# Branches on the number of blocks, put in another order with a hint ahead of each far jump, in an attention, mixture-of-experts and MLP kernel

## The chip, the cores and the metric

The kernel runs on one core of a Trainium2 chip. The metric is the device time of one execution in microseconds (us); of several runs the median counts. The engines are named as the profile names them: PE (TensorE, matrix products), ACT (ScalarE), DVE (VectorE), POOL (GpSimd), SP (SyncE, which here issues the DMA transfers). A `q` behind an engine's name is its sequencer, which runs branches, loads of registers and waits.

## What is computed

Three stages, each fed by the one before, all in float32: attention of 2 x 8 heads over 576 positions with a learned bias by position; a layer of eight experts, of which each of the 1152 tokens goes to one; and a last MLP over all tokens. Cut to what matters for the change:

```python
def _moe_ref(x, w_gate, w1, w2, capacity):      # x (1152, 512), E = 8, F = 1024, capacity 288
    ...
    expert_idx = np.argmax(logits, axis=1)
    gate_w = probs[np.arange(N), expert_idx]
    ...
    for i in range(N):
        e = expert_idx[i]
        if counts[e] < capacity:
            disp[e, counts[e]] = x[i]
            ...
            keep[i] = True
    h = np.maximum(np.einsum('ecd,edf->ecf', disp, w1), 0.0)
    y = np.einsum('ecf,efd->ecd', h, w2)
    out = np.zeros((N, D), dtype=np.float32)
    for i in range(N):
        if keep[i]:
            out[i] = gate_w[i] * y[expert_idx[i], pos[i]]

def _moe2_ref(x, w_in, w_out):                  # 512 -> 2048 -> 512
    h = x @ w_in
    g = np.maximum(0.01 * h, h)
    return g @ w_out
```

A token that its expert has no room for has a row of zeros in the output: these are the blank rows.

## The kernel before

One function, `tile_attention_moe_mlp`, records the instructions of all engines in the order in which it is written; each engine runs its own in that order, and where two engines meet, one waits on a semaphore. PE takes a float32 matrix in two halves: `P[:, 0]` is the value rounded by ACT (L676), `P[:, 1]` what is left (L677, by DVE or POOL), and each product is three matmuls (L860, L861, L862).

After attention the tokens are sorted by expert and cut into blocks: big ones of `CAPB` = 288 tokens and small ones of `CAPS` = 64. How many of each there are depends on the tokens, so their number is read at run time, from `ints`, as `ends[0]` (the end of the bigs) and `ends[1]` (the end of the smalls). The input timed has two big blocks and one small one.

A big block is eight calls of `big_step` (L1041), four for the first product of the expert and four for the second. Step j converts the weight tile of step j + 2 (`split`, L1038, by way of `wsplit`, L675) and runs the 24 matmuls of its own tile. An expert has eight weight tiles of 512 KB, which SP loads (`wdma`, L672) into the buffers R8[0] to R8[7] (`raw` and `w` in the trace). Block 0 stands in a straight line (the loop from L1153). In its last step the tokens of the next blocks, `xr` and `xsr`, are transposed on PE (`prep_at`).

Behind block 0, SP issues three transfers of 768 KB that write zeros from the tile `pre` over all of `out` (`prefill(out, ...)`, L1157 and L1158, by way of L150). Then all engines load `ends` (L1159) and branch:

- L1160, `ends[0] > 1`: into `big(1)`, else past it. `big(i)` (L1055) is a recursion that is unrolled when the program is built: `If(ends[0] > i + 1)` (L1058) holds the eight steps of block i as a middle one and, inside, the whole of `big(i + 1)`; its `Else` (L1067) holds the steps of block i as the last big one, which also load the first small expert. For two big blocks L1058 is false for i = 1, and the engines jump over the code of all longer cases to the `Else` of the outermost nest.
- L1162, `ends[1] > ends[0]`: into `small(0)` (L1074), which has the same form with L1129. For one small block L1129 is false for i = 0, and the engines jump over the nest again.

POOL needs no wait before these branches and takes them early; PE, ACT, DVE and SP each come to them when their own work is done.

Then comes the last MLP, `chunk(0)`: its weights, `wo`, come in 16 tiles of 1 MB as 64-bit numbers (`w<-wo`, L684, 13 loads there), DVE turns each to float32 in three steps (L690, L692, L694), and ACT and POOL split them like the experts'. A loop over i from 0 to 12 runs the products; at its end `emit` multiplies by the gate and POOL scatters the rows to `out` (L1197).

Of the kernel before, what the change touches and what calls it, by code (L numbers as in the profile page):

```python
# [51 lines left out]
NLST = 17  # L52
# [22 lines left out]
def tile_attention_moe_mlp(ctx, tc, qc, kc, vc, wpk, cst, ctok, cap, wm, wo, out):  # L75
    nc = tc.nc
# [20 lines left out]
    R8 = CS[:, S // 4 : S // 4 + S // 16]  # L97
# [574 lines left out]
    def wdma(src, raw):  # L672
        nc.sync.dma_start(raw, src)
# [44 lines left out]
    def wsrc(e, j):  # L718
        return wm[bass.ds(e, 1), j].rearrange("a p f -> p (a f)")
# [103 lines left out]
    def tail_part(fa):  # L823
# [151 lines left out]
        def bval(l, i, f, engines):  # L975
            o = 3 * (NLST * l + i) + (2, 0, 1)[f]
            return nc.values_load(blk[0:1, o : o + 1], engines=engines, min_val=0, max_val=(E_N - 1, SROWS - CAPB, T - 1)[f])
# [3 lines left out]
        def load_x(base):  # L981
            for t, n in xtiles:
                nc.sync.dma_start(xr[t][0:n], srt[sl_(base + 128 * t, n), 0:DM])
# [68 lines left out]
            if prep and j >= 5:  # L1052
                prep_x(j - 5)

        def big(i):  # L1055
            xbase, base = bval(0, i, 1, [SP]), bval(0, i, 2, [ACT, DVE, SP])
            copy_id(xbase, base, CAPB)
            with tc.If(ends[0] > i + 1) as more:  # L1058
                if i + 2 < NLST:
                    ne = bval(0, i + 1, 0, [SP])  # L1060
                    load_x(bval(0, i + 1, 1, [SP]))
                    for j in range(8):
                        big_step(j, base, nc.gpsimd, prep=True)
                        for q in ((), (), (0, 1), (2, 3), (4,), (5,), (6,), (7,))[j]:
                            wdma(wsrc(ne, q), R8[q])
                    big(i + 1)
            with more.Else():  # L1067
                ne = bval(1, 0, 0, [SP])
                for j in range(8):
                    big_step(j, base, nc.gpsimd)  # L1070
                    if j > 2:
                        wdma(wsrc(ne, j - 3), R8[j - 3])

        def small(i):  # L1074
            e, xbase, base = bval(1, i, 0, [SP]), bval(1, i, 1, [SP]), bval(1, i, 2, [ACT, DVE, SP])
            for q in (5, 6, 7):
                wdma(wsrc(e, q), R8[q])
            copy_id(xbase, base, CAPS)
            pend_h = []

            def turn():
                j, hb = pend_h.pop()
                pt = gs[gi[0] % 3]
                gi[0] += 1
                for a in range(2):
                    nc.tensor.matmul(pt[:, CAPS * a : CAPS * a + CAPS], hb[:, 128 * a : 128 * a + 128], II, start=True, stop=True)
                v = pt[:, 0 : 2 * CAPS].rearrange("p (a n) -> p a n", a=2)
                d = hs[:, 2 * j : 2 * j + 2]
                nc.scalar.activation(d[:, :, 0:CAPS], v, AF.Relu)
                nc.vector.scalar_tensor_tensor(out=d[:, :, CAPS:], in0=v, scalar=0.0, in1=d[:, :, 0:CAPS].bitcast(F32),  # L1090
                                               op0=ALU.max, op1=ALU.subtract)

            def step(j, last):
                if j < 6 or not last:
                    split((j + 2) % 8, nc.gpsimd if j in SG else nc.vector)
                Pt = Ps[j % 4]
                if j < 4:
                    ps = gs[gi[0] % 3][:, 0:256]
                    gi[0] += 1
                    for k in range(NP):  # L1100
                        for t in range(2):
                            nc.tensor.matmul(ps, xsh[:, k], Pt[:, t, 256 * k : 256 * k + 256], start=k + t == 0, stop=k == NP - 1 and t == 1)
                    nc.scalar.copy(hsb[j % 2], ps)
                    if pend_h:
                        turn()
                    pend_h.append((j, hsb[j % 2]))
                else:
                    for kk in range(2):
                        k = 2 * (j - 4) + kk
                        for t in range(2):  # L1110
                            for i in range(2):
                                o = 512 * kk + 256 * i
                                nc.tensor.matmul(acs[i][:, 0:256], hs[:, k], Pt[:, t, o : o + 256], start=k + t == 0, stop=k == 7 and t == 1)
                    if j == 4:
                        turn()

            def finish(last):
                nc.scalar.copy(ysb[:, 0:256], acs[0][:, 0:256])
                nc.vector.tensor_copy(ysb[:, 256:512], acs[1][:, 0:256])
                for i in range(2):  # L1120
                    ps = gs[gi[0] % 3]
                    gi[0] += 1
                    for k in range(2):
                        nc.tensor.matmul(ps[:, CAPS * k : CAPS * k + CAPS], ysb[:, 256 * i + 128 * k : 256 * i + 128 * k + 128], II, start=True, stop=True)
                    nc.vector.tensor_copy(y[:, 2 * i : 2 * i + 2, sl_(base, CAPS)], ps[:, 0 : 2 * CAPS].rearrange("p (k n) -> p k n", k=2))
                if last:
                    yprep(0)

            with tc.If(ends[1] > ends[0] + i + 1) as more:  # L1129
                if i + 2 < NLST:  # L1130
                    ne = bval(1, i + 1, 0, [SP])
                    load_xs(bval(1, i + 1, 1, [SP]))
                    for j in range(8):
                        step(j, False)
                        if j > 2:
                            wdma(wsrc(ne, j - 3), R8[j - 3])
                        if j == 6:
                            prep_xs()
                    finish(False)
                    small(i + 1)  # L1140
            with more.Else():
                for j in range(8):
                    step(j, True)
                finish(True)

        fa = fa[:2] + fin_b(*fa)
        run(fill(mb[:, 0], kbt[0:nr, :, 1], kbt[0:nr, :, 1], ALU.add))
# [2 lines left out]
            for t in PX[m + 1]:  # L1150
                prep_xs() if t == 3 else prep_x(t)

        for j in range(8):  # L1153
            big_step(j, 0, nc.vector, post0, last=prep_at)
            if j == 6:
                prep_at(-1)
        for i in range(3):  # L1157
            prefill(out, 3 * i, 3)  # L1158
        ends = [nc.values_load(ints[0:1, 4 + i : 5 + i], min_val=0, max_val=2 * NBLK) for i in range(2)]  # L1159
        with tc.If(ends[0] > 1):  # L1160
            big(1)
        with tc.If(ends[1] > ends[0]) as more:  # L1162
            small(0)
        with more.Else():
            yprep(0)

        osb = [rt.tile([128, DM], F32, name=f"osb{i}", tag="xn", bufs=XB) for i in range(-(-MC // 128))]
        kt = nc.values_load(ints[0:1, 1:2], min_val=0, max_val=T)
# [31 lines left out]
        def chunk(c):  # L1200
            w = MCS[c]
            groups = [(t, min(128, w - 128 * t)) for t in range(-(-w // 128))]
            cv = convs()
            PP = [Ds[i] if c == 0 and i < 2 else Ps[i % 4] for i in range(16)]
            if c:
                for i in range(3):
                    wdma(wsc[i], raws[i])
                yprep(c)
            for i in range(3, 5):
                conv_start(i)  # L1210
            if c:
                for i in range(2):
                    wsplit(raws[i], PP[i], nc.vector)
            for i in range(13):
                if i + 2 < 16:
                    wsplit(spare if c == 0 and i == 0 else raws[(i + 2) % 4], PP[i + 2], nc.gpsimd)
                q = PO[i]
                if q < 8:
                    for g in (0, 2, 1, 3):
                        up_half(PP[i], 2 * q + g // 2, w // 2 * (g % 2), w // 2)  # L1220
                        if g != 3:
                            next(cv, None)
                else:
                    for kk in range(2):
                        for t, n in groups:
                            down_tok(PP[i], 2 * (q - 8) + kk, t, n)
                            if t == 0:
                                split_h()
                            if 2 * t + kk in DCV:
                                next(cv, None)  # L1230
                if i == 5:
                    for t, n in groups:
                        nc.sync.dma_start(idg[0:n, t], sid[MOF[c] + 128 * t : MOF[c] + 128 * t + n].bitcast(I32))
            wsplit(raws[15 % 4], PP[15], nc.vector)
            for t, n in groups:
                for i in range(13, 16):
                    for kk in range(2):
                        down_tok(PP[i], 2 * (PO[i] - 8) + kk, t, n)
                emit(t, n)
# [114 lines left out]
```

## Time and profile before

| | us |
|---|---|
| median of 3 runs | 423.31 |
| lowest and highest | 421.41, 426.03 |
| span of the profiled execution, first to last instruction | 422.7 |
| its busy PE, DVE, ACT, POOL | 384.0, 307.7, 241.3, 138.3 |

One page describes one execution. Busy time is what an engine's instructions took; branches, waits and the issuing of transfers are not counted in it. The views behind the page say more: a list of an engine's waits names the instruction that waited and what released it ("issue" where nothing that the profile shows did); the rows of a source line give the length of each kind of instruction of that line, branches (COMPARE_BRANCH) too; a timeline gives the instructions of an engine with the idle time ahead of each in brackets; windows give busy time, granted TensorE clock (1.00 is the 2.4 GHz level) and DMA traffic of chosen stretches. Matmuls overlap in the pipeline, so the distance of their starts, and not their length, says how fast they run.

### The profile page before, as it was taken

How to read it: one execution, taken by the hardware profiler on the slowest of the kernel's cores; microseconds unless marked ns; L12 is line 12 of the kernel's file. 1: busy time of each engine (PE TensorE's matmuls, PEld its weight loads, DVE VectorE, ACT ScalarE, POOL GpSimd, SP SyncE). 2: the span in 40 equal slices, each digit the busy share in tenths (PEclk: the TensorE clock that was granted, in tenths of full speed). 3: DMA queues.
4: the chain of work that ended last, by engine and by line, in shares of the span. 5: the costliest groups of instructions: out<-in, count | busy, mean ns of one | idle time of the engine just before them, and what ended most of it. 6: DMA issues, size and time to landing. Idle time of an engine off the chain costs nothing. (4 is left out here: it accounts for less than half of the span.)

```text
span 422.7 us, 8338 instructions
## 1 busy us (share of the span) xinstructions
PE 384.0 (91%) x2926; PEld 317.9 (75%) x2926; DVE 307.7 (73%) x731; ACT 241.3 (57%) x519; POOL 138.3 (33%) x110
## 2 busy tenths in 40 slices
PE   4877999998999999999999976997999999999995
PEld 2235566566788888988889966996888877988783
DVE  5997888798855789799458940205799899999500
ACT  3746898697865877767655852526554512455300
POOL 1443857374100101212332202780122245242221
PEclk9998899999899999999999996999999999999999
DMA  8989498698678938788364469850523356640011
GB/s 202 344 236 309 156 346 303 215 304 257 177 213 302 316 125 258 203 258 241 70 204 189 152 218 362 281 195 6 200 100 101 115 185 200 211 188 2 0 68 54
DMA packets 34371, 83.10 MB, mean 197 GB/s; under 512 B 8479, under 2 KB 8863, under 8 KB 32260
## 3 DMA queue, kind: packets, MB, share of 16 engines
q1 hardware_dynamic: 33188, 79.88, 58.6%
q0 software_dynamic: 1120, 2.48, 1.7%
q8 instruction: 28, 0.46, 0.5%
q14 instruction: 35, 0.29, 0.2%
HBM read 60.29 MB, written 23.20 MB: 197 GB/s over the span
## 5 line engine op out<-in xcount | busy, mean ns | idle before, releaser
L345 DVE CUSTOM_DVE_ANT_0 sv<-St,bt 128x576 f32<-128x576 f32 x72 | 52.9, 751 | 36.0 <-PE St L333 24.1
L677 POOL TENSOR_TENSOR P<-raw,P 128x1024 fp32r<-128x1024 f32 x18 | 45.6, 2535 | 81.6 <-ACT P L676 81.5
L356 ACT ACTIVATE A<-sv,mx 128x576 f32<-128x576 f32 x72 | 59.2, 837 | 3.9 <-DVE mx L345 3.7
L333 PE MATMUL St<-K,Q 128*128 128x320 f32 (+1 forms) x320 | 55.0, 316 | 3.2 <-DVE mx L345 3.2
L333 PEld LDWEIGHTS St<-K,Q 128*128 128x128 f32 x320 | 45.5, 195 | 15.1 <-issue 10.2
L182 PE MATMUL pb<-Gt,WP 128*32 128x272 f32 (+17 forms) x352 | 44.0, 504 | 14.0 <-DVE Gt L165 7.8
L273 POOL TENSOR_TENSOR Q<-qr,Q 128x256 fp32r<-128x256 f32 x22 | 17.1, 777 | 105.9 <-ACT Q L265 64.5
L676 ACT CAST P<-raw 128x1024 fp32r<-128x1024 f32 x27 | 28.3, 1048 | 36.8 <-DVE raw L694 22.7
L165 DVE TENSOR_SCALAR Gt<-WL,bp 128x432 f32<-128x432 f32 (+17 forms) x101 | 48.4, 539 | 0.1
L366 PE MATMUL pt<-CS,A 128*128 128x128 f32 x288 | 42.1, 287 | 0.4 <-ACT bs L193 0.2
L376 ACT COPY AT<-pt 128x512 f32<-128x512 f32 x40 | 23.4, 585 | 32.2 <-PE pt L366 32.1
L366 PEld LDWEIGHTS pt<-CS,A 128*128 128x128 f32 x288 | 38.7, 207 | 1.0 <-ACT bs L193 0.4
L182 PEld LDWEIGHTS pb<-Gt,WP 128*32 128x32 f32 x352 | 13.1, 111 | 31.7 <-DVE Gt L165 14.6
L169 POOL TENSOR_SCALAR Gt<-WL,bp 128x528 f32<-128x528 f32 (+12 forms) x17 | 33.8, 1993 | 9.3 <-PE pb L182 9.2
L403 PE MATMUL xp<-AT,V 128*64 128x128 f32 x512 | 36.2, 285 | 0.0
L193 ACT ACTIVATE bs<-pb,CS 128x288 f32<-128x288 f32 (+53 forms) x60 | 27.4, 504 | 12.8 <-PE pb L182 8.3
L860 PE MATMUL g<-yhl,P 128*128 128x304 f32 x96 | 30.2, 315 | 3.8 <-DVE gfa L885 3.8
L1189 PE MATMUL ac<-P,hq 128*128 128x512 f32 (+1 forms) x80 | 31.5, 394 | 0.0
L1187 PE MATMUL ac<-P,hq 128*128 128x512 f32 (+1 forms) x80 | 31.5, 394 | 0.0
L1188 PE MATMUL ac<-P,hq 128*128 128x512 f32 (+1 forms) x80 | 31.5, 393 | 0.0
L403 PEld LDWEIGHTS xp<-AT,V 128*64 128x64 f32 x512 | 28.3, 140 | 4.0 <-issue 0.2
L893 DVE TENSOR_TENSOR hq<-gfa,hq 128x304 fp32r<-128x304 f32 x32 | 28.7, 897 | 1.4 <-ACT hq L892 1.4
(317 smaller groups left out, 909.3 us busy)
## 6 DMA issues: line engine op xcount, KB each, us to landing
bt<-scr SPq DMA_DIRECT2D x24, 576.0 KB, 4.8
w<-wo SPq DMA_DIRECT2D x13, 1024.0 KB, 4.9
scr<-bs SPq DMA_DIRECT2D x36, 295.5 KB, 5.1
raw<-wm SPq DMA_DIRECT2D x14, 512.0 KB, 6.7
w<-wm SPq DMA_DIRECT2D x10, 512.0 KB, 5.8
srt<-pre SPq DMA_DIRECT2D x6, 771.0 KB, 7.8
qr<-qc SPq DMA_DIRECT2D x16, 256.0 KB, 5.6
kr<-kc SPq DMA_DIRECT2D x12, 288.0 KB, 6.7
```

The source lines that it names most:

```text
L165: nc.vector.tensor_scalar(G, src, bp[:, g : g + 1], 0.0, op0=ALU.add, op1=ALU.max)
L169: nc.gpsimd.tensor_scalar(G, src, bp[:, g : g + 1], 0.0, op0=ALU.add, op1=ALU.max)
L182: nc.tensor.matmul(pb[32 * q : 32 * q + 32, 0 : hi - lo], W2, gs[:, q, lo:hi], start=True, stop=True)
L333: nc.tensor.matmul(St[:, o + lo : o + hi], Q[:, h - 2 * p, w, :], K[:, h - 2 * p, lo:hi], start=n == 0, stop=n == len(seq) - 1)
L345: nc.vector.tensor_tensor_reduce(out=sv, in0=St, in1=bt[:, jb], scale=-0.125, scalar=3.0e38, op0=ALU.add, op1=ALU.min, accum_out=mx)
L356: nc.scalar.activation(A[:, :, j], sv, AF.Exp, bias=mx, scale=-1.0, accum_out=rs[:, col : col + 1])
L366: nc.tensor.transpose(pt[:, 128 * t : 128 * t + 128], A[:, 128 * t : 128 * t + 128, j], ident)
L403: nc.tensor.matmul(xp[64 * j : 64 * j + 64, p, :], V[:, t, 64 * h : 64 * h + 64], AT[:, j, 128 * t : 128 * t + 128], start=False, stop=t = ...
L677: eng.tensor_tensor(out=P_[:, 1], in0=raw, in1=P_[:, 0].bitcast(F32), op=ALU.subtract)
L1187: nc.tensor.matmul(ps, hh, wh, start=k == 0, stop=False)
L1188: nc.tensor.matmul(ps, hh, wl, start=False, stop=False)
L1189: nc.tensor.matmul(ps, hl, wh, start=False, stop=k == F2 // 128 - 1)
```

## The change

Three things change; the arithmetic does not.

1. The first question on the bigs is now `ends[0] > 2` (labelled "bigs"). Its body holds the long cases, its `Else` the case of two big blocks, with `If(ends[0] > 1)` inside. Likewise `ends[1] > ends[0] + 1` (labelled "smalls") holds the cases of two and more small blocks, and its `Else` those of one and none. For the input timed both questions are false, and the engine jumps to the `Else`.
2. Ahead of step 7 of block 0 stands a prefetch hint for the branch "bigs", and ahead of step 7 of the last big block one for "smalls", each on PE, ACT, DVE and SP and each "LikelyTaken". They are wrapped in `If(1)`.
3. The three fills of `out` leave their place behind block 0 and go into the loop of `chunk(0)`, at the end of the passes i = 2, 4 and 6.

```diff
-        def big(i):
+        def hint(label):
+            tc.mark_branch_hint_location(label, "LikelyTaken", [PE, ACT, DVE, SP])
+
+        def big_head(i):
             xbase, base = bval(0, i, 1, [SP]), bval(0, i, 2, [ACT, DVE, SP])
             copy_id(xbase, base, CAPB)
-            with tc.If(ends[0] > i + 1) as more:
...
-            with more.Else():
-                ne = bval(1, 0, 0, [SP])
+            return base
+
+        def big_mid(i, base):
+            if i + 2 < NLST:
+                ne = bval(0, i + 1, 0, [SP])
+                load_x(bval(0, i + 1, 1, [SP]))
                 for j in range(8):
+                    big_step(j, base, nc.gpsimd, prep=True)
+                    for q in ((), (), (0, 1), (2, 3), (4,), (5,), (6,), (7,))[j]:
+                        wdma(wsrc(ne, q), R8[q])
+                base = big_head(i + 1)
+                with tc.If(ends[0] > i + 2) as more:
+                    big_mid(i + 1, base)
+                with more.Else():
+                    big_last(base)
+
+        def big_last(base, mark=None):
+            ne = bval(1, 0, 0, [SP])
+            for j in range(8):
+                with tc.If(1) if mark and j == 7 else ExitStack():
+                    if mark and j == 7:
+                        hint(mark)
                     big_step(j, base, nc.gpsimd)
                     if j > 2:
                         wdma(wsrc(ne, j - 3), R8[j - 3])
...
-        for j in range(8):
+        for j in range(7):
             big_step(j, 0, nc.vector, post0, last=prep_at)
-            if j == 6:
-                prep_at(-1)
-        for i in range(3):
-            prefill(out, 3 * i, 3)
+        prep_at(-1)
+        with tc.If(1):
+            hint("bigs")
+            big_step(7, 0, nc.vector, post0, last=prep_at)
         ends = [nc.values_load(ints[0:1, 4 + i : 5 + i], min_val=0, max_val=2 * NBLK) for i in range(2)]
-        with tc.If(ends[0] > 1):
-            big(1)
-        with tc.If(ends[1] > ends[0]) as more:
-            small(0)
+        with tc.If(ends[0] > 2, label="bigs") as more:
+            big_mid(1, big_head(1))
         with more.Else():
-            yprep(0)
+            with tc.If(ends[0] > 1):
+                big_last(big_head(1), "smalls")
+        with tc.If(ends[1] > ends[0] + 1, label="smalls") as more:
+            small(0, True)
+        with more.Else():
+            with tc.If(ends[1] > ends[0]) as one:
+                small(0, False)
+            with one.Else():
+                yprep(0)
...
+                if c == 0 and i in (2, 4, 6):
+                    prefill(out, 3 * (i // 2 - 1), 3)
                 if i == 5:
```

In `small` the two halves of the old `If` become `mid()` and `end()`, and a call with `more` given takes one of them without a branch.

How the engines' orders change, first on PE ahead of step 7 of block 0 (`ac` and `g` are PSUM tiles, `hq` the halves of the hidden values, `P` a split weight tile, `xr` the next block's tokens):

```order
 L861 MATMUL ac_3169<-hq_3147,P_3141 128x288
 L862 MATMUL ac_3169<-hq_3145,P_3141 128x288
+L1178 UNCONDITIONAL_BRANCH
+L1380 BRANCH_PREFETCH_HINT
 L860 MATMUL ac_3166<-hq_3145,P_3142 128x288
 L861 MATMUL ac_3166<-hq_3147,P_3142 128x288
```

The hint (L1380 is the kernel's entry, to which it is booked) now stands ahead of the 24 matmuls of step 7; six of them come before the first transposes of `xr`. At the end of the same step, on PE:

```order
 L861 MATMUL ac_3169<-hq_3147,P_3142 128x288
 L862 MATMUL ac_3169<-hq_3145,P_3142 128x288
-L1159 TENSOR_LOAD ints x2
-L1160 COMPARE_AND_BRANCH
-L1058 COMPARE_AND_BRANCH
+L1178 UNCONDITIONAL_BRANCH
+L1181 TENSOR_LOAD ints x2
+L1182 COMPARE_AND_BRANCH
 L860 MATMUL g_3160<-xhl_3039,P 128x288
 L861 MATMUL g_3160<-xhl_3039,P 128x288
```

Two branches, of which the second was the far jump of this input, have become one, with the far jump as its first question.

On ACT around the same place (`xhl` and `xsh` are the next blocks' tokens in halves, `y` the old block's result):

```order
 L676 CAST P<-raw 128x1024
 L1027 COPY y<-pre 128x1440
+L1178 UNCONDITIONAL_BRANCH
+L1380 BRANCH_PREFETCH_HINT
 L676 CAST P<-raw 128x1024
 L920 COPY y<-ac_3166 128x288
```

ACT's hint stands ahead of the conversion that belongs to step 7. On SP, in the loop of the last MLP (`w` are the two 1 MB buffers), the change has:

```order
L684 DMA w_3144<-wo 128x2048
L150 DMA out<-pre 128x3x512
L684 DMA w_3143<-wo 128x2048
L684 DMA w_3144<-wo 128x2048
L150 DMA out<-pre 128x3x512
L684 DMA w_3143<-wo 128x2048
L1263 DMA idg<-sid 128x2 x4
```

There, before, the loads followed each other; the first of these rows is the fifth load, and a third fill follows the tenth. Where the fills came from, on SP behind block 0, before:

```order
L673 DMA w_3144<-wm 128x1024
L150 DMA out<-pre 128x3x512 x3
L1159 TENSOR_LOAD ints
L1159 ISA x2
L1159 TENSOR_LOAD ints
L1159 ISA x2
L1160 COMPARE_AND_BRANCH
```

The three transfers stood between the last weight load and the branches, and these now follow each other directly, but for the end of the `If(1)`.

## Rows read from the trace of the kernel before

**Rows 1.** The page: span, and busy time by engine

```profile
span 422.7 us, 8338 instructions
PE 384.0 (91%) x2926; PEld 317.9 (75%) x2926; DVE 307.7 (73%) x731; ACT 241.3 (57%) x519; POOL 138.3 (33%) x110
```

**Rows 2.** Waits of PE, 245:310: us in total, times, longest

```profile
PE g L860 <- issue: 5.1, 1, 5.1
PE g L1102 <- issue: 2.1, 1, 2.1
...
PE g L1102 <- DVE P L677: 0.9, 1, 0.9
```

**Rows 3.** L1058's branches: ns min/median/max, first and last start us

```profile
L1058 PEldq COMPARE_BRANCH  x2: 188/3056/5923, 251.6 to 282.7; - x2
L1058 ACTq COMPARE_BRANCH  x2: 38/44/50, 253.6 to 284.5; - x2
```

**Rows 4.** The same for the branch of L1129

```profile
L1129 PEldq COMPARE_BRANCH  x2: 292/2150/4008, 283.2 to 299.6; - x2
...
L1129 ACTq COMPARE_BRANCH  x2: 38/46/55, 285.3 to 301.0; - x2
L1129 DVEq COMPARE_BRANCH  x2: 47/55/63, 286.7 to 303.5; - x2
```

**Rows 5.** The same for the branch of L1162, PE

```profile
L1162 PEldq COMPARE_BRANCH  x1: 92/92/92, 282.9 to 282.9; - x1
```

**Rows 6.** Timeline of ACT: start, us, idle before it and releaser

```profile
245.06 1.04 ACT L676 CAST P<-raw 128x1024 fp32r<-128x1024 f32 x1
...
258.93 1.05 ACT L676 CAST P<-raw 128x1024 fp32r<-128x1024 f32 x1 [6.61 <-DMA w<-wm]
```

**Rows 7.** L676's semaphore instruction on ACT, 253 to 259.5 us

```profile
L676 ACTq EVENT_SEMAPHORE  x1: 17/17/17, 258.9 to 258.9; - x1
```

**Rows 8.** DMA of 251.6 to 257.7 us, and the fill's issues

```profile
DMA packets 656, 2.43 MB, mean 399 GB/s; under 512 B 66, under 2 KB 66, under 8 KB 654
...
out<-pre SPq DMA_DIRECT2D x3, 768.0 KB, 14.3
```

**Rows 9.** DMA of 283.1 to 287.3 us

```profile
DMA packets 115, 0.04 MB, mean 8 GB/s; under 512 B 112, under 2 KB 112, under 8 KB 112
```

**Rows 10.** Windows: PE, PEld, DVE, ACT, POOL busy, PEclk, DMA share, GB/s

```profile
254.80:257.70 2.90, 0.00 (x0) 0.00 (x0) 0.00 (x0) 0.00 (x0) 0.00 (x0) 0.51 1.04 387
257.70:261.70 4.00, 3.96 (x16) 3.99 (x17) 0.19 (x1) 1.46 (x2) 1.59 (x1) 0.50 0.92 320
261.70:272.30 10.60, 10.60 (x81) 10.60 (x81) 3.01 (x7) 5.28 (x9) 7.16 (x4) 1.00 0.87 274
...
287.40:301.00 13.60, 11.73 (x88) 10.64 (x88) 8.97 (x14) 8.77 (x17) 0.00 (x0) 1.00 0.12 34
```

**Rows 11.** Timeline of PE, 245 to 249 us

```profile
245.09 0.29 PE L860 MATMUL ac<-hq,P 128*128 128x288 f32 x1
...
247.78 0.66 PE L728 MATMUL g<-CS,xr 128*128 128x128 f32 x4 [1.74 <-DMA xr<-srt]
```

**Rows 12.** Timeline of ACT at the second jump

```profile
288.14 1.05 ACT L676 CAST P<-raw 128x1024 fp32r<-128x1024 f32 x1 [3.27 <-PE g L1102]
```

**Rows 13.** Timeline of DVE there

```profile
289.99 2.36 DVE L677 TENSOR_TENSOR P<-raw,P 128x1024 fp32r<-128x1024 f32 x2 [4.26 <-PE g L1102]
```

**Rows 14.** Loads of the last MLP's weights (L684): landing

```profile
DMA to landing us min/median/max: 4.7/4.9/8.3
```

**Rows 15.** Timeline of DVE, 342 to 354 us: third conversion step

```profile
342.05 1.23 DVE L694 SCALAR_TENSOR_TENSOR raw<-w,raw 128x1024 uint32<-128x1024 uint32 x1
...
345.18 3.31 DVE L694 SCALAR_TENSOR_TENSOR raw<-w,raw 128x1024 uint32<-128x1024 uint32 x1
...
350.38 3.30 DVE L694 SCALAR_TENSOR_TENSOR raw<-w,raw 128x1024 uint32<-128x1024 uint32 x1
```

**Rows 16.** Waits of PE, 300 to 423 us

```profile
PE g L860 <- DVE gfa L885: 3.8, 5, 1.0
```

## What the change should do: a prediction

> **What bounds the kernel now.** I read the page first: 422.7 us of span, TensorE (PE) busy for 91% of it [rows 1]. So time can only be won where PE stands still or runs slowly. The change touches the stretch from 245 to 310 us, and I next read what PE waits for there [rows 2]. The two longest waits, 5.1 and 2.1 us, have "issue" as their releaser: nothing that the profile shows ended them, no data and no semaphore. The reader should then look at the branches by line. PE's sequencer ran that of L1058 twice: once in 188 ns, once, from 251.6 us on, in 5923 ns [rows 3]. It ran L1129 once in 292 ns and once, from 283.2 us on, in 4008 ns [rows 4]. L1162, which does not jump far here, took 92 ns [rows 5]. The two long ones are the two PE waits: PE drains the matmuls already issued and has nothing more until the branch comes through, the first at 251.65 + 5.92 = 257.6 us.
>
> The other engines show the same hole as idle time, not as a long branch. ACT's branch of L1058 has at most 50 ns and comes at 253.6 us [rows 3], yet after it ACT does nothing until 258.93. The timeline blames a DMA for those 6.61 us, but the semaphore instruction just ahead of that work lasted 17 ns, so the semaphore was already up [rows 6, 7]. What holds all of them, as I read it, is the arrival of the instructions at the far end of the jump. In the first jump the DMA engines carried 399 GB/s, in the second 8 GB/s [rows 8, 9]: with traffic about, the same kind of jump took 5.92 us on PE, in quiet 4.01.
>
> Behind the first hole lies a second cost. From 254.8 to 257.7 us PE has no work and the clock is granted at 0.51; from 257.7 to 261.7 it has work without a gap at 0.50 (the 1.2 GHz level), 16 matmuls in 4.0 us; from then on, at 1.00, 81 take 10.6 us, 0.131 us each [rows 10].
>
> **The change part by part.**
>
> *One far jump per kind of block.* For this input (two big blocks, one small one) the old kernel too takes one far jump for the bigs (L1058 false) and one for the smalls (L1129 false); the branches ahead of them fall through. So the reordering removes no far jump here; it makes the two jumps ones that a hint can name. A new branch in place costs 0.09 us by L1162 [rows 5]; those around step 7 of block 0 lie ahead of a wait of 1.74 us that PE has for xr until 247.78 [rows 11], the others behind matmuls that are already queued. I take 0; uncovered, four would be 0.4 us.
>
> *The hint at the first jump.* No hint runs in the trace of before, so its worth is bounded by nothing (0) and by the whole fetch coming ahead of time. Its lead decides. On PE it stands six matmuls ahead of the wait for xr, at 245.09 us [rows 11], and the jump is reached at 251.65: 6.6 us, more than the 5.92 that the fetch took under load. ACT's hint stands ahead of a conversion that runs at 245.06 [rows 6], 8.5 us before its branch at 253.6; DVE's stands ahead of the subtraction that follows this conversion. SP's lead is shorter, about the time of its last two weight loads, but its next duty, the first loads for the small block, is for work some 20 us later. So I take the whole fetch: of PE's 5.1 us, 0.1 stays: -5.0. What is late next is nothing: ACT comes free with PE, the first two weight tiles of the new block are converted in the old block's last steps, and the others are used one by one, a step of 24 matmuls (24 x 0.131 = 3.1 us) apart.
>
> The Trainium skill, "Runtime: NRT & Kernel Launch", section "Instruction fetch mechanics", says that prefetch is purely sequential and that a taken branch to a target outside the current window forces a DMA fetch. The trace agrees with its second half (5923 and 4008 ns against 188 and 292); no run here yet shows the first. By that first half no hint could help, and the sum would end at about 422.3 us, the rival without effect below.
>
> *The clock.* In this trace the granted clock fell, in this part, behind PE's empty stretch of 5.1 us alone; after the second, of 2.1 us, it is at 1.00 [rows 10]. Without the first the 16 matmuls take 16 x 0.131 = 2.1 us instead of 4.0: -1.9. If half of the hole stayed, the fall could stay with it: 0 at that end.
>
> *The second jump.* PE's hint stands ahead of the last step of the last big block, 24 x 0.131 = 3.1 us of matmuls before the jump; PE's sequencer also runs ahead of its matmuls, at the first jump by 1 us (reached at 251.65, last matmul over at 252.6). So its lead is about 4.1 us against a quiet fetch of 4.01: barely enough, and up to 1 us may stay. ACT and DVE, whose hints stand ahead of the same step's first work, matter more, since the small block begins with conversions: ACT begins P at 288.14 after 3.27 us idle, DVE its half at 289.99 after 4.26 [rows 12, 13], and PE then waits 0.9 us for that half [rows 2]. ACT's branch came at 285.3, DVE's at 286.7 [rows 4]. Without a fetch ACT could start P some 0.4 us behind its branch, at 285.7 (-2.4), and DVE at 287.1, behind P's 1.05 us and its own branch (-2.9); PE's own hole is 2.1. I take -2.4, between PE's and DVE's, with 0 and -2.9 as ends.
>
> *The fill of blank rows.* Before, three fills of 768 KB were issued right behind the weights and landed 14.3 us after issue [rows 8]. They delay nothing on PE's path: weights and PE's fetch were queued ahead of them, and the fetch was over at 257.6, less than 6 us after the first fill's issue. Taking them away there: 0, at best the 1.9 us by which the loaded fetch exceeded the quiet one, if the hint leaves it. In the new place one fill stands behind the fifth, the seventh and the tenth of the 1 MB loads of the last MLP. At 399 GB/s [rows 8] a fill is 1.9 us of traffic and a load 2.6 us; a load lands 4.7 to 4.9 us after issue [rows 14], and the cycle of the conversions that it feeds is 5.2 us (345.18 to 350.38) [rows 15]: 4.5 us of traffic fit. Were a load late all the same, DVE's third conversion step, which takes 3.3 us there against 1.23 just before [rows 15], holds 2.1 us that I read as a wait for another engine and which the lateness would only fill. PE's largest wait in the MLP is 3.8 us in all on DVE [rows 16]. Ends: 0 and 3 x 1.9 = 5.7; by the slack I take +0.2.
>
> Sum against the profiled span: 422.7 - 5.0 - 1.9 - 2.4 + 0.2 = 413.6. The median of the runs, 423.31, lies 0.6 above the span, so **414.2 us**.
>
> **The rivals.**
> - *The hints do nothing.* Both fetches stay; the first may shrink towards the quiet 4.01, since the fills no longer share the DMA engines: 0 to -1.9, and the MLP's +0.2. I say 422.3 (421.4 to 423.5). For it: no row of before shows a hint at work. Chance 0.12. The skill's sentence on sequential prefetch, cited above, stands on this side.
> - *Only the first hint works*: the second comes too late, on ACT and DVE too. 422.7 - 5.0 - 1.9 + 0.2 + 0.6 = 416.6. Chance 0.13.
> - *One engine stays late at the first jump*: PE finds its instructions, but ACT or DVE fetches for 2 to 4 us more and PE waits for it. 417 to 419. Against it: ACT's lead is longer than PE's. Chance 0.09.
> - *Slower: the fills hold up the weights of the last MLP.* If a fill took there what it took before, 14.3 us, with the next load stuck behind it, that load, issued 5.2 us after the last, would come 14.3 - 5.2 = 9.1 us late, 7.0 less the slack of 2.1; two such give 14.0, so 414.2 + 14.0 = 428. It decides from 423.3 - 414.2 = 9.1 us, that is 4.6 us of PE's time for each of two fills. Against it: the 14.3 us came from three fills behind the weights, on DMA engines that were full. Chance 0.06.
>
> **How the numbers follow.** Both hints work: 0.60. Its own range is 412.0 to 416.3: the second jump between -2.9 and about -0.5, the fills up to 1 or so, and the spread of the runs of before (421.41 to 426.03). The range 411.8 to 419.0 takes in this, the second and the third rival, 0.60 + 0.13 + 0.09 = 0.82. The bound of "faster" is 1% below 423.31, 419.1, since 1% is about what a measurement of this kernel can tell from no change: so faster has the same 0.82, the case without effect gives 0.12 within 1%, the fills 0.06 slower.
>
> **What would show it.** In the new trace PE's branches of L1182 and L1187 at 0.3 us or less; no wait "<- issue" of PE over 0.5 us between 245 and 300 us; the granted clock at 1.00 through 250 to 260 us; ACT's and DVE's first work right behind their branches. A branch still at 4 to 6 us means that the hint does nothing there. A short branch and a new wait of PE on ACT, DVE or POOL at the head of a block means that another engine's fetch is late. Waits of PE on DVE far above 3.8 us in the MLP, or weight loads there that land over 7 us after issue, would show the fills. What would most likely make me wrong: that a hint is lost when other instructions are fetched after it, or that it brings fewer instructions than the engine uses up before the stream behind them arrives.

## The result: slower, and the profile after

| | us |
|---|---|
| before, median of 16 runs | 423.36 |
| changed, median of 16 runs | 430.1 (425.75 to 433.2) |
| ratio | 1.0129, 95% interval 1.0099 to 1.0159 |
| span of the profiled execution, changed | 426.7 (its own time 428.59) |

The change costs 1.3%, where 2.1% less was forecast. Ratios here and below leave out runs more than 1.5% above the fastest of the same kernel (two here, six of e1's ten, four of e5's ten, one of e7's ten), so a median can lie further from 423 than its ratio says. The profiled execution of the change is one of its shorter ones: it shows 4.0 us of the 6.7 between the medians. Around a span lie 1.8 to 1.9 us (428.59 against 426.7), not the 0.6 that I took.

The page of the changed kernel, span and busy time:

```profile
span 426.7 us, 8344 instructions
...
PE 385.8 (90%) x2926; PEld 321.0 (75%) x2926; DVE 309.2 (72%) x731; ACT 241.1 (56%) x519; POOL 138.8 (33%) x110
```

The waits of PE from 245 to 310 us, to be laid beside [rows 2]:

```profile
PE g L1099 <- ACT hy L1116: 3.6, 1, 3.6
PE g L860 <- DVE hq L876: 2.0, 1, 2.0
PE g L860 <- DVE y L918: 1.5, 1, 1.5
```

Both waits "<- issue" are gone. In their place PE waits for ACT and DVE. The branches of lines L1182 ("bigs"), L1185 (`ends[0] > 1`) and L1187 ("smalls"), as [rows 3, 4] show them for before:

```profile
L1182 PEldq COMPARE_BRANCH  x1: 2402/2402/2402, 250.9 to 250.9; - x1
L1182 ACTq COMPARE_BRANCH  x1: 74/74/74, 252.4 to 252.4; - x1
...
L1185 PEldq COMPARE_BRANCH  x1: 73/73/73, 253.4 to 253.4; - x1
...
L1185 ACTq COMPARE_BRANCH  x1: 55/55/55, 257.6 to 257.6; - x1
...
L1187 PEldq COMPARE_BRANCH  x1: 1079/1079/1079, 279.5 to 279.5; - x1
...
L1187 ACTq COMPARE_BRANCH  x1: 69/69/69, 281.4 to 281.4; - x1
```

PE's two far jumps shrank from 5.92 and 4.01 us to 2.40 and 1.08. ACT's did not. L1185 stands at the far end of the first jump (so the two branches of before did not become one: a second follows, in place). It shows when an engine arrives there: ACT at 257.6, 5.2 us after its branch at 252.4, and likewise DVE 4.8 us (253.2 to 258.0) and SP 5.1 us (250.3 to 255.4) after theirs, but PE after 2.5. ACT's timeline (start, us, idle before it), as in [rows 6, 12]:

```profile
258.65 1.04 ACT L676 CAST P<-raw 128x1024 fp32r<-128x1024 f32 x1 [6.80 <-SPq L1380]
...
285.71 1.04 ACT L676 CAST P<-raw 128x1024 fp32r<-128x1024 f32 x1 [4.52 <-DMA sid<-pat]
```

6.80 us idle behind the first jump against 6.61 before, 4.52 behind the second against 3.27. The windows (columns as in [rows 10]) show what PE does meanwhile:

```profile
253.60:260.60 7.00, 5.03 (x36) 4.82 (x36) 0.49 (x2) 1.95 (x4) 0.76 (x1) 1.00 0.60 171
...
281.40:287.08 5.68, 2.04 (x18) 1.84 (x17) 0.69 (x2) 1.37 (x3) 0.00 (x0) 1.00 0.07 9
287.08:293.80 6.72, 6.72 (x31) 6.72 (x32) 5.23 (x7) 4.77 (x10) 0.00 (x0) 0.50 0.00 0
```

At the second jump PE does 2 us of work, stands for 3.6 us until ACT has converted, and then runs 6.7 us at a granted clock of 0.50. The fall that stood behind the first jump before now stands behind the second. In the last MLP, PE's wait from 300 us on, to be laid beside [rows 16]; DVE's waits for the 1 MB weight loads from 300 to 400 us, of which before shows none; and the landing of these loads, beside [rows 14]:

```profile
PE g L860 <- DVE gfa L885: 6.0, 3, 3.6
```

```profile
DVE raw L690 <- DMA w<-wo: 4.3, 4, 1.4
```

```profile
DMA to landing us min/median/max: 4.7/6.2/8.2
```

The following table is worked out from PE's timelines of all kernels that follow: the idle time at the first jump, the last big block (from the start of its first matmul to that of its last), the idle time at the second jump, the small block, and the MLP from its first matmul to the end of the span. What comes ahead of the first jump (248.7 to 254.8 us) is left out.

| kernel | jump 1 | block 1 | jump 2 | small | sum of these | MLP |
|---|---|---|---|---|---|---|
| before | 5.3 | 27.2 | 2.3 | 13.7 | 48.5 | 121.7 |
| changed | 1.7 | 27.6 | 0.0 | 19.1 | 48.4 | 126.2 |
| e3_fill_moved | 5.8 | 28.0 | 3.0 | 13.2 | 50.0 | 126.0 |
| e2_no_hint | 5.8 | 28.0 | 3.8 | 13.7 | 51.3 | 125.9 |
| e4_reorder | 6.0 | 26.7 | 2.4 | 15.6 | 50.7 | 122.1 |
| e1_fill_back | 0.1 | 32.1 | 0.0 | 18.8 | 51.0 | 122.1 |
| e5_hint_pe | 1.8 | 29.8 | 0.8 | 16.5 | 48.9 | 122.1 |
| e6_hint_others | 5.5 | 27.6 | 3.5 | 13.7 | 50.3 | 121.6 |
| e7_hint_early | 0.0 | 32.0 | 0.0 | 19.6 | 51.6 | 122.6 |
| e8_near | 0.0 | 25.3 | 0.0 | 12.4 | 37.7 | 124.3 |
| e9_fill_early | 5.4 | 26.8 | 3.1 | 13.7 | 49.0 | 122.1 |
| e10_near_fill_mlp | 0.0 | 25.3 | 0.0 | 12.4 | 37.7 | 129.3 |
| e11_near_fill_early | 0.0 | 25.3 | 0.0 | 12.4 | 37.7 | 124.4 |

Each row is one execution. Before, e3 and e9 run the same code up to the MLP, and their sums are 48.5, 50.0 and 49.0, so a difference of 1.5 us between two sums says nothing; the row of e1 is one of its longer runs, of 429.81. Between before and changed the stretch of the jumps is level, and the MLP is 4.5 us longer.

### The profile page after: what moved, and what is told of

It reads as the page before. It is cut to its first block, busy times and chain, and to the rows that moved or that the text cites. A ratio compares the mean times of both kernels' runs of the same rounds, so it can differ in the third digit from the quotient of the medians.

```text
span 426.7 us, 8344 instructions
## 1 busy us (share of the span) xinstructions
PE 385.8 (90%) x2926; PEld 321.0 (75%) x2926; DVE 309.2 (72%) x731; ACT 241.1 (56%) x519; POOL 138.8 (33%) x110
## 5 line engine op out<-in xcount | busy, mean ns | idle before, releaser
L677 POOL TENSOR_TENSOR P<-raw,P 128x1024 fp32r<-128x1024 f32 x18 | 44.7, 2488 | 88.7 <-ACT P L676 88.7
L333 PE MATMUL St<-K,Q 128*128 128x320 f32 (+1 forms) x320 | 53.5, 309 | 3.3 <-DVE mx L345 3.2
L333 PEld LDWEIGHTS St<-K,Q 128*128 128x128 f32 x320 | 43.9, 189 | 15.4 <-issue 9.7
L676 ACT CAST P<-raw 128x1024 fp32r<-128x1024 f32 x27 | 28.3, 1047 | 40.1 <-DVE raw L694 24.3
L182 PEld LDWEIGHTS pb<-Gt,WP 128*32 128x32 f32 x352 | 13.2, 112 | 32.8 <-DVE Gt L165 14.4
L169 POOL TENSOR_SCALAR Gt<-WL,bp 128x528 f32<-128x528 f32 (+12 forms) x17 | 34.7, 2043 | 9.3 <-PE pb L182 9.2
L860 PE MATMUL g<-yhl,P 128*128 128x304 f32 x96 | 30.6, 319 | 6.2 <-DVE gfa L885 6.0
L193 ACT ACTIVATE bs<-pb,CS 128x288 f32<-128x288 f32 (+53 forms) x60 | 27.3, 501 | 13.2 <-PE pb L182 8.6
L862 PE MATMUL g<-yhl,P 128*128 128x304 f32 x96 | 29.7, 309 | 0.0
```

Of the source, the lines that this page charges most:

```text
L169: nc.gpsimd.tensor_scalar(G, src, bp[:, g : g + 1], 0.0, op0=ALU.add, op1=ALU.max)
L182: nc.tensor.matmul(pb[32 * q : 32 * q + 32, 0 : hi - lo], W2, gs[:, q, lo:hi], start=True, stop=True)
L333: nc.tensor.matmul(St[:, o + lo : o + hi], Q[:, h - 2 * p, w, :], K[:, h - 2 * p, lo:hi], start=n == 0, stop=n == len(seq) - 1)
L677: eng.tensor_tensor(out=P_[:, 1], in0=raw, in1=P_[:, 0].bitcast(F32), op=ALU.subtract)
```

## The experiments

Two theories stood first. Theory F: the fills delay the weight loads of the last MLP, and that is the loss. Theory R: the loss lies in the order or the hints. Four kernels cross fills and hints.

**e3_fill_moved**: the kernel before, with the fills moved and nothing else.

```diff
-        for i in range(3):
-            prefill(out, 3 * i, 3)
...
+                if c == 0 and i in (2, 4, 6):
+                    prefill(out, 3 * (i // 2 - 1), 3)
```

> The kernel before with only the fills moved into the last MLP. Theory F: slower than before by 4 to 6 us, 427 to 430, with DVE waiting on w<-wo loads. Theory R: within 1 us of before, 422 to 424.5.

Measured: 429.67 us, ratio 1.0159 (1.0087 to 1.0231). The move of the fills alone makes as much as the whole change. Loads in short windows, each with its time to landing (the last number): in before the one issued at 343.31 us, in this kernel the same load, at 342.69, with the fill behind it, and the next, at 347.90:

```profile
w<-wo SPq DMA_DIRECT2D x1, 1024.0 KB, 4.7
```

```profile
w<-wo SPq DMA_DIRECT2D x1, 1024.0 KB, 6.2
out<-pre SPq DMA_DIRECT2D x1, 768.0 KB
...
w<-wo SPq DMA_DIRECT2D x1, 1024.0 KB, 7.3
```

The load ahead of the fill lands 1.5 us later, the one behind it 2.6. DVE's timeline (start, us, idle before it) and POOL's in that stretch:

```profile
344.56 3.31 DVE L694 SCALAR_TENSOR_TENSOR raw<-w,raw 128x1024 uint32<-128x1024 uint32 x1
349.01 0.69 DVE L690 TENSOR_SCALAR raw<-w 128x1024 uint32<-128x1024 uint32 x1 [1.14 <-DMA w<-wo]
349.73 3.31 DVE L692 SCALAR_TENSOR_TENSOR raw<-w,raw 128x1024 uint32<-128x1024 uint32 x1
353.08 1.23 DVE L694 SCALAR_TENSOR_TENSOR raw<-w,raw 128x1024 uint32<-128x1024 uint32 x1
...
366.90 0.69 DVE L690 TENSOR_SCALAR raw<-w 128x1024 uint32<-128x1024 uint32 x1 [1.10 <-DMA w<-wo]
367.51 0.47 DVE L885 TENSOR_TENSOR gfa<-g,gfa 128x304 f32<-128x304 f32 x1
```

```profile
349.10 2.85 POOL L677 TENSOR_TENSOR P<-raw,P 128x1024 fp32r<-128x1024 f32 x1 [2.32 <-ACT P L676]
```

The 2.1 us that I had read as slack in L694 did not take up the delay. They moved to L692, the operation that now falls beside POOL's: it starts at 349.73, POOL ends at 351.95, and L692 ends at 353.04, 1.1 us behind POOL. DVE stands while POOL works, and that price is paid once in each cycle wherever the load lands. The Trainium skill, "SBUF — State Buffer", section "SBUF: two separate sides", states that a DVE operation with two SBUF inputs and a GpSimd operation that reads SBUF hold their shared ports exclusively, and that the loser blocks fully; L692 and L694 have two inputs, POOL's L677 reads `raw` and `P`, and the trace agrees. At 366.90 the second cost shows: L690 stands 1.10 us for its load, and L885, for which PE waits, is queued behind it on DVE. In before the same L885 came at 364.67:

```profile
364.67 0.46 DVE L885 TENSOR_TENSOR gfa<-g,gfa 128x304 f32<-128x304 f32 x1
```

Counted from the first matmul of the MLP that is 63.63 us, and 67.07 here: 3.4 us later, so the waits of the passes before have added up in it. PE's timeline has the wait:

```profile
368.03 0.62 PE L860 MATMUL g<-yhl,P 128*128 128x304 f32 x1 [3.94 <-DVE gfa L885]
```

Its windows show the granted clock at 0.50 right behind this wait:

```profile
367.80:371.20 3.40, 3.17 (x12) 3.17 (x13) 3.40 (x6) 1.22 (x3) 0.00 (x0) 0.50 0.83 294
```

**e1_fill_back, e2_no_hint, e4_reorder**: the change with its fills put back behind block 0; the change without its hints; and the change with both, so the order of the branches alone.

```diff
 e1, e4
+        for i in range(3):
+            prefill(out, 3 * i, 3)
         ends = ...
...
-                if c == 0 and i in (2, 4, 6):
-                    prefill(out, 3 * (i // 2 - 1), 3)
 e2, e4
-            hint("bigs")
...
-                    if mark and j == 7:
-                        hint(mark)
```

> The changed kernel with the three fills put back behind block 0; order of branches and hints as changed. Theory F (the fills delay the weight loads of the last MLP): its profile had four waits of DVE on w<-wo loads, 1.2 + 0.6 + 1.1 + 1.4 = 4.3 us, and waits of PE on gfa 2.2 us above before; these go, landing of w<-wo returns to about 4.9 us, and the time falls by 4 to 6 us, to 424 to 426. Theory R (the loss lies in the new order or the hints, the fills are hidden): no change against the changed kernel, about 430.

> The changed kernel without its hints, fills in the last MLP as changed. If the hints shorten PE's two jumps (2.4 and 1.1 us in the changed kernel against 5.9 and 4.0 before) and this reaches the end, PE's branches return to 4 to 6 us and the time is 3 to 6 us above the changed kernel, 433 to 436. If what PE gains is given back to ACT and DVE, whose work behind the jumps began as late as before, the branches return to 4 to 6 us and the time stays within 2 us of the changed kernel.

> Only the new order of the branches: no hints, fills behind block 0. Both theories on the fills expect the time of before for the far jumps, since there are two of them either way: 422.5 to 424.5, PE's branches at 4 to 6 us. If the new order itself costs something, it is slower by 1 to 4 us, and shows at the jumps of ACT, DVE or SP.

Measured: e2 429.81 (ratio 1.0147, 1.0090 to 1.0205), e4 423.82 (1.0003, 0.9978 to 1.0029), e1 429.04 with ratio 0.9973 (0.9924 to 1.0023). The order costs nothing that can be told from zero. Without hints the change is as slow as with them. With fills back, the hints still win nothing: three runs of e1 lie at 421, the other seven from 426.3 to 430.5. Its ratio counts four of the ten, its median of all ten is 5.6 us above that of before, and none of them lies in the 424 to 426 that theory F expected. What speaks for theory F is the rest: e3 and e2, with the fills moved, are slow, e4 is not, and the MLP of e1 is back at 122.1. It leaves open why PE's shorter jumps are worth nothing. The profile of e1 is of a run of 429.81; PE's waits in it:

```profile
PE g L860 <- DVE hq L876: 4.5, 1, 4.5
PE g L728 <- DMA xr<-srt: 4.2, 2, 2.8
PE g L1099 <- ACT hy L1116: 3.3, 1, 3.3
```

PE waits where ACT's and DVE's first results of the block are due. So it does in the other kernels with PE's hints: for ACT's `hy` and DVE's `hq` 3.6 and 2.0 us in the changed kernel above, 4.7 and 4.5 in e7, 1.5 and 2.6 in e5.

**e5_hint_pe, e6_hint_others**: e1 with hints on PE alone, and on the other three alone.

```diff
-            tc.mark_branch_hint_location(label, "LikelyTaken", [PE, ACT, DVE, SP])
+            tc.mark_branch_hint_location(label, "LikelyTaken", [PE])                # e5
+            tc.mark_branch_hint_location(label, "LikelyTaken", [ACT, DVE, SP])      # e6
```

> New order, fills behind block 0, hints on PE alone. Theory P (only PE's hints bring anything; the run with all hints and the fills put back had PE's branches at 0.4 and 1.2 us and ACT's and DVE's work behind the jumps as late as without hints): no difference from that run, fast runs at 421, PE's branches at 0.4 to 2.4 and at 1.2 us. Theory Q (the hints on ACT, DVE and SP matter, for better or worse): the time or the delay of ACT behind its branches moves by over 1 us against that run.

> New order, fills behind block 0, hints on ACT, DVE and SP and none on PE. Theory P: like the order alone, 423.8, PE's branches at 4 to 6 us, ACT idle 5 us or more behind its first jump and 2.5 or more behind its second. Theory Q: ACT's and DVE's idle time behind the jumps shrinks.

Measured: e5 422.83 (ratio 0.9985, 0.9949 to 1.0021), with runs at 420 to 423 and at 427 to 430 like e1; e6 423.84 (1.0032, 1.0002 to 1.0063), with all runs from 422.7 to 425.1 like e4. Theory P holds, but for e5's second branch, which took 2.46 us and not 1.2. In e6 PE's branch takes 6212 and 5178 ns, and ACT is idle 7.73 us behind the first jump. The branch behind the first jump says it directly, in e4 (no hints) and in e6:

```profile
L1181 ACTq COMPARE_BRANCH  x1: 45/45/45, 249.9 to 249.9; - x1
...
L1184 ACTq COMPARE_BRANCH  x1: 40/40/40, 255.1 to 255.1; - x1
```

```profile
L1184 ACTq COMPARE_BRANCH  x1: 74/74/74, 249.2 to 249.2; - x1
...
L1187 ACTq COMPARE_BRANCH  x1: 55/55/55, 255.0 to 255.0; - x1
```

ACT needs 5.2 us without a hint and 5.8 with one; DVE 5.5 and 6.0, SP 6.1 and 5.7. The instruction fetches fit this. The profile has two queues for them and does not say whose they are; by when their packets come, I read q8 as PE's and q14 as that of the others. From 236 us to the branch on ACT, q14 carries the same two packets in e4 and in e6:

```profile
q14 instruction: 2, 0.02, 0.4%
```

```profile
q14 instruction: 2, 0.02, 0.7%
```

On q8, in e4 there is one fetch from 240 to 252.6 us, that is until 4.1 us into PE's branch of 248.5; in e5, with PE's hint, there are two from 240 to 249:

```profile
q8 instruction: 1, 0.02, 0.5%
```

```profile
q8 instruction: 2, 0.03, 1.3%
```

The second fetch of e5 starts at 248.9, as PE's branch does, which then still takes 2.5 us: against e4 the hint brought it forward by some 4 us, not all the way ahead of the jump. In e1, where the branch took 0.39 us, the second fetch starts 6.7 us ahead of it. In e7 below there is only one between the hint and the branch, and the branch is as short; so the count alone does not show which fetch holds the target.

**e7_hint_early**: all hints, some four steps of a block earlier, fills behind block 0.

```diff
-        for j in range(7):
+        for j in range(4):
             big_step(j, 0, nc.vector, post0, last=prep_at)
-        prep_at(-1)
         with tc.If(1):
             hint("bigs")
-            big_step(7, 0, nc.vector, post0, last=prep_at)
+            for j in range(4, 8):
...
```

(and likewise ahead of step 3 of the last big block)

> All hints, fills behind block 0, each hint some four steps of a block earlier: ahead of step 4 of block 0, and ahead of step 3 of the last big block. If ACT's and DVE's hints failed for want of lead, their first work now stands right behind their branches and the time is 414 to 418. If hints bring nothing on these engines whatever the lead, the time is that of the run with all hints and the fills put back, 421 to 430.

Measured: 426.73, ratio 1.0088 (1.0047 to 1.0129), slower than the order alone. PE's branches and ACT's first work behind them:

```profile
L1191 PEldq COMPARE_BRANCH  x1: 393/393/393, 249.8 to 249.8; - x1
...
L1196 PEldq COMPARE_BRANCH  x1: 366/366/366, 281.0 to 281.0; - x1
```

```profile
258.14 1.04 ACT L676 CAST P<-raw 128x1024 fp32r<-128x1024 f32 x1 [7.44 <-DMA out<-pre]
...
288.41 1.04 ACT L676 CAST P<-raw 128x1024 fp32r<-128x1024 f32 x1 [5.63 <-DMA sid<-pat]
```

With more lead PE's fetch is hidden whole, at both jumps, and ACT is as late as ever: lead is not what ACT's hint lacks. And the kernel is no faster for it: PE now stands in one long wait at the head of each block, 4.5 and 4.7 us where it stood 5.1 and 2.1 before, and the clock is at 0.50 behind both:

```profile
257.80:264.60 6.80, 4.33 (x18) 4.33 (x19) 1.74 (x4) 3.94 (x7) 4.70 (x2) 0.50 0.60 229
...
288.50:295.30 6.80, 5.52 (x26) 5.52 (x27) 4.67 (x6) 5.23 (x9) 0.00 (x0) 0.50 0.00 0
```

Why e7 is slower than the order alone is not shown: the profile of e4 has two such stretches at 0.50 too (251.6 to 258.4 and 285.7 to 292.6), and its sum in the table is 50.7 against 51.6.

**e8_near**: no hints, and no far jump from block 0 to the last MLP. One question, `ends[0] * 64 + ends[1] == 131` (two big blocks, one small), has the usual case in its body, in a row with the last MLP, so that each engine runs on into it; the `Else` keeps all other cases, by the branches of the change, with a copy of the MLP; `rest` is the last MLP. The fills stand behind block 0.

```diff
+        with tc.If(ends[0] * 64 + ends[1] == 2 * 64 + 3) as short:
+            big_last(big_head(1))
+            small(0, False)
+            rest()
+        with short.Else():
...
+            rest()
```

> No hints and no far jump in the timed path: one question on both numbers of blocks (two big and one small) ahead of everything, whose body holds the last big block, the small block and the last MLP in a row, and whose Else holds all other cases with a second copy of the MLP; fills behind block 0. If it is the far jumps of all engines that cost time at both places, PE's waits of 5.1 and 2.1 us behind a branch go, ACT and DVE begin right behind the branch, the clock does not fall there, and the time is 422.7 - 5.0 - 1.9 - 2.4 = 413.4 of span, 413 to 416. If the tokens, the weights or the conversions hold the next block anyway, PE's waits come back under other names and the time is 419 or more.

Measured: **413.92**, ratio 0.9805 (0.9742 to 0.9868). The waits of PE from 246 to 300 us, all of them, the branch on PE, and ACT's first work behind it:

```profile
PE g L860 <- ACT yhl L913: 0.4, 1, 0.4
PE g L1137 <- ACT hy L1131: 0.3, 1, 0.3
PE ac L1126 <- DVE P L677: 0.2, 1, 0.2
```

```profile
L1264 PEldq COMPARE_BRANCH  x1: 90/90/90, 248.4 to 248.4; - x1
```

```profile
250.69 1.05 ACT L676 CAST P<-raw 128x1024 fp32r<-128x1024 f32 x1 [2.04 <-PE g L862]
```

From the first jump to the MLP it takes 37.7 us instead of 48.5. The MLP is 2.6 us longer. Of these only 0.4 lie ahead of its last matmul: 3.4 us at a granted clock of 0.50 (287.4 to 290.8) cost some 1.7, and shorter waits, PE's for `gfa` 2.8 us against 3.8 among them, give most of it back. The other 2.2 lie behind the last matmul (403.5), from where the span takes 7.5 us to its end instead of 5.2. A far jump of this input is left there:

```profile
L1260 PEldq COMPARE_BRANCH  x2: 3907/4274/4641, 399.2 to 403.7; - x2
```

The first of the two has its like in before (3547 ns on L1243, under queued matmuls). The second, 4.64 us from 403.7, is in e8, e10 and e11 alone; I read it as the way out past the `Else`. So the tokens, weights and conversions were ready in time, and the far jumps of all engines together were the whole cost of the two holes. Only this input was timed; every other one now goes to the `Else`.

**e9_fill_early, e10_near_fill_mlp, e11_near_fill_early**: before with the fills in passes 0, 1 and 2 of the MLP; e8 with the fills in passes 2, 4 and 6; e8 with them in 0, 1 and 2.

```diff
+                if c == 0 and i < 3:                       # e9, e11
+                    prefill(out, 3 * i, 3)
+                if c == 0 and i in (2, 4, 6):              # e10
+                    prefill(out, 3 * (i // 2 - 1), 3)
```

> The kernel before with the fills in the last MLP's passes i = 0, 1 and 2, behind the third, fourth and fifth load, where the trace of before has 8.35 us from one load to the next; in the passes 4 and 6 it has 5.2, and there the kernel with only the fills moved had DVE waiting 4.2 us for weights and an MLP of 126.0 instead of 121.7 us. If a fill costs what it and a load together overrun the cycle of the conversions, DVE waits for no load here and the time is within 1 us of before, MLP 121.5 to 122.5. If a fill costs wherever it shares the DMA engines with those loads, the MLP stays at 124 us or more and the time is 2 to 6 us above before.

> The kernel without far jumps in the timed path (413.9 us) with the fills in the passes 2, 4 and 6 of the MLP as in the change. If the price of the fills is a matter of the MLP alone, it adds the same 4 to 6 us: 418 to 420. If the fills were dear only beside the jumps' late start, less than 2: 413 to 416.

> The kernel without far jumps with the fills in the passes 0, 1 and 2. If the cycle of 8.35 us hides them, 412.5 to 415, level with the fills behind block 0 (413.9) or, should the fills there hold up the next block's weights, up to 1 us better; if not, 416 or more.

Measured: e9 423.63 (ratio 1.0026, 0.9992 to 1.0061), e10 418.69 (0.9870, 0.9791 to 0.9949), e11 **413.5** (0.9766, 0.9707 to 0.9826). The same three fills cost nothing that can be told from zero where the loads come 8.35 us apart (issues of before at 311.17, 319.54, 327.89 and 336.24), and 4.8 us (418.69 - 413.92) in the passes 2, 4 and 6. There the first fill still has 8.35 us to the next load, and the second and third stand where loads come 5.2 apart (343.31 to 348.51, 358.96 to 364.17); in e3 all four waits of DVE for loads come behind these two. e11 cannot be told from e8. DVE's wait for the loads, in e9 and in e10:

```profile
DVE raw L690 <- DMA w<-wo: 0.2, 1, 0.2
```

```profile
DVE raw L690 <- DMA w<-wo: 5.0, 4, 1.6
```

## Why the prediction was wrong, point by point

- *What bounds the stretch* was right: far jumps wait for instructions. Without those two, e8 measured 413.92, near the sum of the prediction (413.6 of span, 414.2 us). That the number fits so well is in part luck: the stretch gained 10.8 us where 9.3 was forecast, the MLP gave 2.6 back, and by its ratio to before, 0.9805, e8 would stand at 415.1.
- *The hint at the first jump*: right on PE, where it brings the fetch ahead (5.92 to 2.40 us, and 0.39 with more lead). The step that failed is "ACT comes free with PE". On ACT, DVE and SP the hint brought nothing (e6: 5.7 to 6.0 us from branch to branch, 5.2 to 6.1 without), and on ACT and DVE nothing at the longer lead either (e7: 5.3 and 5.9). The third rival had this mechanism; I gave it 0.09 because ACT's lead was longer than PE's, and lead was not the point. The Trainium skill, "Runtime: NRT & Kernel Launch", section "Instruction fetch mechanics", has prefetch as purely sequential: the rows of ACT, DVE and SP agree, those of PE do not, and the measurement decides.
- *The clock*: the fall behind the first jump went, as forecast (1.00 in the window from 253.6 on). At the first jump that and the shorter hole leave a gain of 3.2 us: 1.7 + 27.6 against 5.3 + 27.2 (without PE's hints these two sum to 32.2 to 33.8 in the table, with them to 29.3 to 32.2). PE's waits for ACT and DVE took the rest of the 5.0 + 1.9 that were forecast.
- *The second jump*: -2.4 was forecast and +3.1 came (19.1 against 2.3 + 13.7; the kernels without PE's hints have 16.0 to 18.0). PE lost its 2.1 us of idle, but ACT began 4.5 us after its last copy instead of 3.3 (4.5 too in e2 and e4, without hints), PE waited 3.6 us for it, and the clock fell there instead. I did not ask what happens to a clock when one engine of a chain arrives early and the others do not.
- *The fills*: +0.2 forecast, 4.3 us of MLP measured (e3, 126.0 against 121.7), and 6.3 between the medians. Two steps failed. "4.5 us of traffic fit" into a cycle of 5.2 counted bytes at full rate and took the load's landing as fixed; in the run the load beside the fill landed 1.5 us later and the next 2.6. And the "slack" of 2.1 us was DVE standing behind POOL, a part of its full cycle. The fourth rival, at 0.06, had the mechanism. That its 428 lies near the 430.1 is luck: it took the full gains of the hints, which did not come, and 14.0 us for the fills, where 4.3 came in the MLP; it priced two late loads at 7.0 where four came, by up to 1.4 us each in the change. At their old place the fills cost nothing, as taken: without them there PE's first jump took 6.52 us in e3, against 5.92. Two slips change nothing: a fill at 399 GB/s is 2.0 us of traffic and not 1.9, and the low end of the first rival, with its own +0.2, is 421.6. The fourth rival's turning point, 4.6 us per fill, took the gains of the hints for granted; without them any cost in the MLP decides.

What stays open: why the hints bring nothing on ACT, DVE and SP; what parts the two groups of runs that e1 and e5 show (420 to 423 and 426 to 430), of which the clock is a trace: from 240 to 310 us the profile of e1, a run of 429.81, has four stretches at 0.50, some 24 us, the first of them ahead of the jump, behind waits for `xr` of 2.8 and 1.4 us, and that of e5, a run of 422.78, has two, some 7 us; why ACT's idle time at the second jump lies between 3.2 and 5.6 us in kernels with the same work; and some 2 us of the 6.3 between the medians, since the profiled execution of e3 (428.18) is shorter than its median.

## What to carry to other kernels

A far jump costs every engine its own fetch: hiding it on the busiest engine alone moves the wait to the next one, so look for the first work, or the next branch, of each engine behind the jump. Putting the usual case in the way of the instruction stream, so that nobody jumps, was worth 2.0 to 2.3% here and needed no hint; the way out past the other cases is still a jump, 2.2 us at the end here, and I have not tried to take it away. Before a long operation is called slack, see what ends it, and before a transfer is moved beside a stream of loads, see whether their cycle has room (8.35 us had, 5.2 had not, for a load of 1 MB and a fill of 768 KB).

## What the runs showed of the hardware that I had not expected

- A prefetch hint shortened PE's far jump, from 4.0 to 6.7 us to 0.37 to 2.5 (0.37 and 0.39 in e7, the earliest). On ACT, DVE and SP the first jump took 5.7 to 6.0 us with a hint (e6) and 5.2 to 6.1 without (e4), and no more packets came on q14 ahead of it.
- Hiding the jumps of the busiest engine alone won nothing: e7, with PE's two hidden, is 0.9% slower than before. PE stands 4.5 and 4.7 us instead of 5.1 and 2.1, and each of the new waits is followed by 6.8 us at a granted clock of 0.50.
- A fill of 768 KB delayed the weight load issued ahead of it as well as the one behind: 6.2 and 7.3 us to landing instead of 4.7.
